# A recurrent attention and a routed expert layer on one core: q and k turned by products alone, gathers and weight loads in another order

## The chip, the cores and the metric

The kernel runs on one core of one Trainium2 chip. The metric is the device time of one execution in microseconds (us), lower is better. The kernel before was timed three times: 344.85, 353.26 and 343.91 us, a median of 344.85.

## What is computed

Two layers follow each other. The first is attention with a decaying state, for 4 batches, 8 heads, 768 positions and 64 values a head; the second sends each of the 3072 rows that come out of it either past the experts or to one of eight.

```python
def _attn_ref(q, k, v):                 # q, k, v: [4, 8, 768, 64]
    gamma = 1.0 - 2.0 ** (-5.0 - np.arange(H, dtype=np.float32))
    for t in range(S):
        state = gamma[None, :, None, None] * state + np.einsum('bhd,bhe->bhde', k[:, :, t], v[:, :, t])
        y[:, :, t] = scale * np.einsum('bhd,bhde->bhe', q[:, :, t], state)

def _moe_ref(x, w_skip, w_gate, w1, w2):   # x: [3072, 512], w1: [8, 512, 1024], w2: [8, 1024, 512]
    do_compute = x @ w_skip > 0
    out = x.copy()
    xc = x[do_compute]
    logits = xc @ w_gate
    e_idx = np.argmax(logits, axis=1)
    gate_w = softmax(logits)[e_idx]
    for e in range(E):
        mask = e_idx == e
        h = np.maximum(xc[mask] @ w1[e], 0.0)
        y[mask] = gate_w[mask, None] * (h @ w2[e])
    out[do_compute] = xc + y
```

## The kernel before, in words

**The attention stage** works on 16 pairs of heads (four batches of four pairs; index `i`), each with 768 positions in chunks of 128. One engine each has its part: SyncE loads the k, q and v of pair `i+4`; GpSimd (POOL) multiplies k and q of pair `i+2` with powers of the decay (`scale_rows`, line 94, tiles `ks` and `qs`); TensorE computes; ScalarE (ACT) and VectorE (DVE) carry results out of PSUM. The order of the instructions on each engine is the order in which the code is written (`manual_schedule`). One pass of the loop at line 433 issues on TensorE:

- `kv_states(i)`, line 232: 20 products of `ks` with v, 64x64, into the four 64x64 quarters of the array in turn. VectorE makes states `St` of them (lines 241 and 244).
- `scores(i, 0)`, line 270: 12 products. VectorE masks them into `ATm` (line 276).
- `rows_t(i+1, 0)`, lines 213 and 215: turns the k and a third of the q of the next pair, so that the position comes to lie along the free axis: 32 blocks of 64x64. ScalarE copies the result to `QKT` (line 217).
- `values(i-1)`, line 293, 24 products; ScalarE and VectorE copy a half each to `xT` (line 299).
- `rows_t(i+1, 1)`: the other 16 blocks.
- `scores(i, 1)` with the products of q and the states (line 250) in between; masked as above.
- `rows_x(i-1)`, line 317: turns the result back and multiplies it with the gate's columns at once. ScalarE copies to `xall` and `Lp`; after each fourth pair it sends the batch's rows to `out` (line 326).

The blocks of `rows_t` go through the four quarters of the array in turn. Where the result lies in the lower half of the PSUM partitions (`o == 0`), the block is turned by a transpose (line 213), otherwise by a product with the identity (line 215); so two transposes and two products take turns. A float32 product is two records in the trace, a transpose is one.

A batch that is complete goes through the gate in three following passes, on VectorE: the choice of the expert (`gate_a`), the place of each row in its expert's list (`gate_count`, `gate_b`, lines 364 to 395), and the table of the lists (`one_hots`, `table`, lines 404 to 420). The last batch does all three behind the last pair.

**The expert stage** begins with `slots`: row numbers (`gi` with empty slots set to row 0, for the gathers; `si` with empty slots set past the end, for the scatters) and the factors `g`. Each expert has 256 slots in two tiles of 128. POOL issues all 16 gathers of rows from `out` (line 498, a tile of its own each, `xg`), and between them the weights of experts 4 to 7 (`load_w`, lines 183 and 186; those of experts 0 to 3 were loaded during the attention). Then for each expert: `layer1` (line 522), `x_tr` of the next expert (lines 508 to 513: to bf16, turned), `layer2` (line 535), and for each of two tiles VectorE's weighted sum `yo` (line 540, four buffers) and POOL's scatter back to `out` (line 543). The scatters are declared free of each other, as they name distinct rows; of the gathers they are not, and since both work on `out`, a scatter waits for all gathers ahead of it. A loop behind this (line 585) takes further passes where an expert has over 256 rows; with these inputs it takes none.

The step from line 213 on is what the first part of the change touches, lines 477 to 563 the second.

Of the kernel before, what the change touches and what calls it, by code (L numbers as in the profile page):

```python
# [18 lines left out]
def kernel(  # L19
# [133 lines left out]
    w8 = poolC.tile([128, NCH * E], FP32, name="w8")  # L153
    vals = poolC.tile([128, NCHT, NV], BF16, name="vals")

    def gate_constants():
        ut_f = poolC.tile([128, 128], FP32, name="ut_f")
        make_upper_triangular(nc, ut_f[:, :], val=1.0, diag=False)
        iota_i = poolC.tile([128, CAP], I32, name="iota_i")
        G_.iota(iota_i[:, :], pattern=[[1, CAP]], base=0, channel_multiplier=0)  # L160
        w8_i = poolC.tile([128, NCH * E], I32, name="w8_i")
        G_.iota(w8_i[:, :], pattern=[[0, NCH], [-1, E]], base=E, channel_multiplier=0)
        chv_i = poolC.tile([128, NCHT], I32, name="chv_i")
        G_.iota(chv_i[:, :], pattern=[[1, NCHT // R], [0, R]], base=0, channel_multiplier=0)
        row_i = poolC.tile([128, NCHT], I32, name="row_i")
        G_.iota(row_i[:, :], pattern=[[0, NCHT // R], [1, R]], base=1, channel_multiplier=R)
        V_.tensor_copy(identb[:, :], ident[:, :])
        V_.tensor_copy(utb[:, :], ut_f[:, :])
        V_.memset(onesb[:, :], 1.0)
        V_.tensor_copy(iotab[:, :], iota_i[:, :])  # L170
        V_.tensor_copy(w8[:, :], w8_i[:, :])
        V_.tensor_copy(vals[:, :, 0], chv_i[:, :])
        V_.tensor_copy(vals[:, :, 1], row_i[:, :])
        V_.memset(Rsum[:, :], 0.0)
        V_.memset(Tsb[:, :], 0.0)
# [21 lines left out]
    def rows_t(i, m):  # L197
# [7 lines left out]
        for j in range(n):  # L205
            w, s_ = divmod(j0 + j, NCH)
            for c in range(2):
                cp = slice(64 * c, 64 * c + 64)
                for h in range(2):
                    o = 64 * (h ^ c)  # L210
                    dst, rows = ps[c][o : o + 64, j * 64 : (j + 1) * 64], (ks, qs)[w][i][cp, s_, h, :]
                    if o == 0:
                        PE.transpose(out=dst, in_=rows, identity=ident[cp, cp])  # L213
                    else:
                        PE.matmul(out=dst, lhsT=rows, rhs=ident[cp, cp], start=True, stop=True, skip_group_check=True)  # L215
        for c in range(2):
            A_.copy(  # L217
                out=QKT[i][:, j0 : j0 + n, 64 * c : 64 * c + 64],
# [214 lines left out]
    for i in range(NU):  # L433
# [6 lines left out]
        scale_rows(i + 2, 1, G_)  # L440
        if i == 0:
            gate_constants()
        for e, which in WEARLY.get(i, ()):
            load_w(e, which, poolW)
        rows_t(i + 1, 1)
# [29 lines left out]
    def slots():  # L475
# [2 lines left out]
        sh = [128, NST, E]  # L478
        tid = poolE.tile(sh, FP32, tag="tid", bufs=1, name="tid")
        V_.scalar_tensor_tensor(out=tid[:, :, :], in0=T[:, :, 0, :], scalar=256.0, in1=T[:, :, 1, :], op0=ALU.mult, op1=ALU.add)  # L480
        gi = poolE.tile(sh, I32, tag="gi", bufs=1, name="gi")
        V_.tensor_scalar(gi[:, :, :], tid[:, :, :], -1.0, 0.0, ALU.add, ALU.max)
        emp = poolE.tile(sh, FP32, tag="emp", bufs=1, name="emp")
        V_.tensor_scalar(emp[:, :, :], T[:, :, 1, :], 0.0, BIG, ALU.is_equal, ALU.mult)
        si = poolE.tile(sh, I32, tag="si", bufs=1, name="si")
# [1 line left out]
        g = poolE.tile(sh, FP32, tag="g", bufs=1, name="g")  # L487
        V_.tensor_tensor(g[:, :, :], T[:, :, 2, :], T[:, :, 3, :], ALU.add)
        V_.tensor_tensor(g[:, :, :], g[:, :, :], T[:, :, 4, :], ALU.add)  # L489
        return gi, si, g  # L490

    gi, si, g = slots()
    xg, xgT = {}, {}

    def gather(e, gi):
        for st in range(NST):
            t = poolE.tile([128, DM], FP32, tag=f"xg{e}_{st}", bufs=1, name="xg")
            G_.indirect_dma_start(  # L498
                out=t[:, :], out_offset=None, in_=out[:, :],
                in_offset=bass.IndirectOffsetOnAxis(ap=gi[:, st, e : e + 1], axis=0), bounds_check=N - 1, oob_is_err=False,  # L500
            )
            xg[e, st] = t

    def x_tr(e):
        xgT[e] = poolE.tile([128, NDB, CAP], BF16, tag="xgT", bufs=2, name="xgT")
# [20 lines left out]
            A_.activation(out=hT[:, 2 * f2 : 2 * f2 + 2, :], in_=ps[:, :, :], func=AF.Relu, bias=0.0, scale=1.0)  # L526
        return hT

    scatters = []

    def layer2(e, hT, si, g, first=False):
        for st in range(NST):
            ps = psE.tile([128, DM], FP32, tag="yps", bufs=2, name="yps2")
            for fb in range(NFB):
# [1 line left out]
                    out=ps[:, :], lhsT=hT[:, fb, st * 128 : (st + 1) * 128], rhs=w2b[e][:, fb, :],  # L536
                    start=(fb == 0), stop=(fb == NFB - 1),
                )
            yo = poolE.tile([128, DM], FP32, tag="yo", bufs=4, name="yo")
            V_.scalar_tensor_tensor(  # L540
                out=yo[:, :], in0=ps[:, :], scalar=g[:, st, e : e + 1], in1=xg[e, st][:, :], op0=ALU.mult, op1=ALU.add
            )
# [2 lines left out]
                in_=yo[:, :], in_offset=None, bounds_check=N - 1, oob_is_err=False,  # L545
            )
            if first:
                for o in scatters:
                    tc.declare_no_dep(sc.ins, o.ins, reason="the slots of a pass name distinct rows")
                scatters.append(sc)  # L550

    late = [(e, w) for e in range(4, E) for w in range(2)]
    for e in range(E):
        gather(e, gi)
        if e >= 1:
            load_w(*late.pop(0), poolX)
    load_w(*late.pop(0), poolX)
    x_tr(0)
    for e in range(E):
        hT = layer1(e)  # L560
        if e + 1 < E:
            x_tr(e + 1)
        layer2(e, hT, si, g, first=True)


    NPASS = (N + CAP - 1) // CAP - 1
# [18 lines left out]
    with tc.For_i(0, n_more) as _:  # L585
        V_.tensor_scalar(posT[:, :], posT[:, :], -float(CAP), None, ALU.add)
        V_.memset(Tsb[:, :], 0.0)
        for b in range(B):
            js = batch_js(b)
            table_add(table(js, one_hots(js, poolE), psE, "cnt", 1))  # L590
        gi2, si2, g2 = slots()
        for e in range(E):
            gather(e, gi2)
        for e in range(E):
            x_tr(e)
            layer2(e, layer1(e), si2, g2)

# [29 lines left out]
```

## Time and profile before

| | us |
|---|---|
| median of three executions | 344.85 |
| lowest, highest | 343.91, 353.26 |
| profiled execution, whole | 348.22 |
| its span in the trace | 346.1 |
| TensorE busy (share of the span) | 269.2 (78%) |
| TensorE's weight loads | 205.9 (60%) |
| VectorE busy | 132.6 (38%) |
| ScalarE busy | 74.2 (21%) |
| GpSimd busy | 90.1 (26%) |

The profile is of one execution, with times in us from the start of its span. Matmuls are pipelined: records overlap, and the pace is read from their starts. The attention stage goes to about 223 us, the expert stage from 232.86 to 336. A share of busy time is a mean over both. The chain of waits is followed back from the last instruction: at each step to what released it, or to the instruction before it on its engine; "issue" is time in which an engine waited for nothing that the profile shows. A wait for several semaphores is put down to the one that came last.

### The profile page before, as it was taken

What the parts mean: (1) busy time and instruction counts of PE and PEld (TensorE: products, weight loads), DVE (VectorE), ACT (ScalarE), POOL (GpSimd) and SP (SyncE); (2) the same over time, 40 slices, a digit from 0 to 9 for tenths busy, and PEclk for the clock granted to TensorE, in tenths of its full rate; (3) what the DMA queues carried; (4) which work ended last, traced back from release to release, by engine and by line L of the source; (5) the groups of instructions that cost most, each with busy time, mean ns of one, the idle gap of its engine ahead of it and who ended that gap; (6) DMA issues with size and microseconds to landing.
All of it is one profiled execution on the core that took longest, in us unless ns stands there. A gap on an engine that the chain in (4) does not pass through costs nothing.

```text
span 346.1 us, 10993 instructions
## 1 busy us (share of the span) xinstructions
PE 269.2 (78%) x4941; PEld 205.9 (60%) x4941; DVE 132.6 (38%) x423; ACT 74.2 (21%) x185; POOL 90.1 (26%) x95
## 2 busy tenths in 40 slices
PE   2999999999799989799999697624998300899960
PEld 1667877887687677577787476513666300466630
DVE  3444324424746532708533607462232001433320
ACT  2110322223132132123132121300222200022220
POOL 2723303321322141111430000007633212322220
PEclk9999989989999899769999878855899955699995
DMA  8995414438852259610589980046999995111110
GB/s 217 272 285 144 135 28 117 140 93 206 283 141 81 62 137 252 197 47 4 102 159 214 258 190 4 2 182 146 235 256 252 245 243 159 64 51 60 50 60 6
DMA packets 45202, 49.99 MB, mean 144 GB/s; under 512 B 2922, under 2 KB 39786, under 8 KB 43104
## 3 DMA queue, kind: packets, MB, share of 16 engines
q0 software_dynamic: 4864, 24.07, 30.2%
q1 hardware_dynamic: 38688, 18.90, 20.4%
q10 hardware_dynamic: 1600, 6.29, 4.6%
q8 instruction: 40, 0.66, 0.8%
q14 instruction: 10, 0.08, 0.1%
HBM read 56.64 MB, written 10.49 MB: 194 GB/s over the span
## 4 chain that ended last, share of the span: by engine, by line
PE 74%; DMA 9%; DVE 8%; issue 6%; ACT 1%; POOL 1%; POOLq 0%; DVEq 0%; ACTq 0%
PE tps L215 17%; PE tps L213 12%; PE atps L270 9%; PE yps L535 8%; PE hps L522 8%; PE yps L293 7%; DMA xg<-out_dram,gi 5%; PE kvps L232 4%; DMA out_dram<-yo,si 3%; PE tps L317 2%; PE yps L250 2%; DVE ATm L276 2%; PE xtp L512 2%; PE tabps L412 1%; DVE xb L508 1%
## 5 line engine op out<-in xcount | busy, mean ns | idle before, releaser
L276 DVE TENSOR_TENSOR ATm<-atps,maskc 128x384 f32<-128x384 f32 x64 | 32.7, 553 | 51.8 <-PE atps L270 51.4
L217 ACT COPY QKT<-tps 128x512 f32<-128x512 f32 (+1 forms) x64 | 27.6, 482 | 109.1 <-PE tps L215 109.1
L94 POOL TENSOR_TENSOR qs<-qw,tq 128x768 f32<-128x768 f32 x15 | 22.4, 1494 | 95.2 <-issue 80.2
L270 PE MATMUL atps<-QKT 64*64 64x128 f32 x768 | 41.6, 298 | 7.0 <-issue 4.7
L526 ACT ACTIVATE hT<-hps 128x512 bf16<-128x512 f32 x32 | 19.1, 597 | 86.3 <-PE hps L522 86.3
L215 PE MATMUL tps<-ident,ks 64*64 64x64 f32 x384 | 35.4, 265 | 0.5 <-issue 0.5
L512 PE MATMUL xtp<-identb,xb 128*128 128x128 bf16 x64 | 7.3, 244 | 36.3 <-DVE xb L508 36.3
L215 PE MATMUL tps<-ident,qs 64*64 64x64 f32 x384 | 35.2, 262 | 0.0
L270 PEld LDWEIGHTS atps<-QKT 64*64 64x64 f32 x768 | 29.5, 144 | 9.5 <-issue 5.3
L498 POOL DMA_INDIRECT xg<-out_dram,gi x16 | 16.3, 1020 | 68.9 <-DVE g L489 50.8
L213 PE MATMUL tps<-ident,ks 64*64 64x64 f32 x192 | 29.3, 259 | 6.2 <-POOL ks L94 6.2
L213 PE MATMUL tps<-ident,qs 64*64 64x64 f32 x192 | 33.1, 256 | 0.9 <-ACT QKT L217 0.9
L94 POOL TENSOR_TENSOR ks<-kw,tk 128x768 f32<-128x768 f32 x16 | 24.0, 1499 | 33.1 <-PE kvps L232 26.1
L522 PE MATMUL hps<-xgT,w1b 128*128 128x256 bf16 x256 | 32.1, 287 | 0.5 <-DVE xgT L513 0.5
L522 PEld LDWEIGHTS <-w1b 128*128 128x128 bf16 x256 | 30.1, 146 | 3.2 <-issue 0.7
L540 DVE SCALAR_TENSOR_TENSOR yo<-yps,g,xg 128x512 f32<-128x512 f32 x16 | 11.9, 750 | 48.7 <-DMA out_dram<-yo,si 28.3
L535 PE MATMUL yps<-w2b,hT 128*128 128x512 bf16 x128 | 30.2, 391 | 0.0
L293 PE MATMUL yps<-ATm,vn 64*64 64x128 f32 x768 | 29.9, 310 | 0.0
L244 DVE TENSOR_TENSOR St<-kvps,St 64x64 f32<-64x64 f32 x128 | 28.4, 222 | 3.0
L543 POOL DMA_INDIRECT out_dram<-yo,si x16 | 15.9, 992 | 48.2 <-DVE yo L540 35.5
L512 PEld LDWEIGHTS <-xb 128*128 128x128 bf16 x64 | 5.0, 121 | 38.1 <-DVE xb L508 38.1
L299 DVE COPY xT<-yps 128x384 f32<-128x384 f32 x16 | 8.9, 557 | 47.8 <-PE yps L293 47.7
(99 smaller groups left out, 319.8 us busy)
## 6 DMA issues: line engine op xcount, KB each, us to landing
w1b<-in_moe_w_dram POOLq DMA_DIRECT2D x8, 1024.0 KB
w2b<-in_moe_w_dram POOLq DMA_DIRECT2D x8, 1024.0 KB, 17.7
kw<-in_k_dram SPq DMA_DIRECT2D x16, 384.0 KB, 5.9
qw<-in_q_dram SPq DMA_DIRECT2D x16, 384.0 KB, 5.7
vn<-in_v_dram SPq DMA_DIRECT2D x16, 384.0 KB, 5.4
out_dram<-xall ACTq DMA_DIRECT2D x4, 1536.0 KB, 13.5
xg<-out_dram,gi POOLq DMA_INDIRECT x16, 12.7
out_dram<-yo,si POOLq DMA_INDIRECT x16, 2.6
```

The lines of the kernel that those rows point to most:

```text
L94: eng.tensor_tensor(o[:, :, :, :], rows, sc, ALU.mult)
L213: PE.transpose(out=dst, in_=rows, identity=ident[cp, cp])
L215: PE.matmul(out=dst, lhsT=rows, rhs=ident[cp, cp], start=True, stop=True, skip_group_check=True)
L217: A_.copy(out=QKT[i][:, j0 : j0 + n, 64 * c : 64 * c + 64], in_=ps[c][:, 0 : 64 * n].rearrange("p (j t) -> p j t", j=n),)
L244: V_.tensor_tensor(st[o : o + 64, ch, :], kv[o : o + 64, :], st[64 - o : 128 - o, ch - 1, :], ALU.add)
L270: PE.matmul(out=ps[t][cp, j, :], lhsT=QKT[i][hp, a * SPB + j, cp], rhs=QKT[i][hp, NCH + R * g : NCH + R * g + R, cp], start=True, stop=True,)
L276: V_.tensor_tensor(out=ATm[i, a][:, t, :, :], in0=ps[t][:, :, :], in1=maskc[:, a * SPB : (a + 1) * SPB, :, :].rearrange("p s r t -> p s (r ...
L293: PE.matmul(out=Y[i, c][64 * h : 64 * h + 64, g, :], lhsT=vn[i][cp, h * G + g, r * D : (r + 1) * D], rhs=ATm[i, a][cp, h ^ c, j, :], start ...
L512: PE.transpose(out=ps[:, db, :], in_=cols[:, db, :], identity=identb[:, :])
L522: PE.matmul(out=ps[:, f, :], lhsT=w1b[e][:, db, :].rearrange("p (c a) -> p a c", a=NFB)[:, fb, :], rhs=xgT[e][:, db, :], start=(db == 0), ...
L526: A_.activation(out=hT[:, 2 * f2 : 2 * f2 + 2, :], in_=ps[:, :, :], func=AF.Relu, bias=0.0, scale=1.0)
L535: PE.matmul(out=ps[:, :], lhsT=hT[:, fb, st * 128 : (st + 1) * 128], rhs=w2b[e][:, fb, :], start=(fb == 0), stop=(fb == NFB - 1),)
```

## The change

First, in `rows_t` the transposes are gone: every block is turned by a product with the identity. Second, the rows of the experts lie in eight fixed tiles `xrows`, two for each of four experts, set to zero once in pass 2 of the attention loop; expert `e` and expert `e + 4` share theirs. The gathers use `si`, so empty slots are left out and keep what was there. Only experts 0 to 3 are gathered at first, with two of the eight late weights in between; behind each expert's scatters stand the gather of the expert four further on, as long as there is one, and two late weights, as long as there are any. Scatters and gathers of this stage are declared free of each other, and `yo` has eight buffers.

```diff
+    xrows = [poolC.tile([128, DM], FP32, name=f"xrows{t}") for t in range(4 * NST)]
...
-                    dst, rows = ps[c][o : o + 64, j * 64 : (j + 1) * 64], (ks, qs)[w][i][cp, s_, h, :]
-                    if o == 0:
-                        PE.transpose(out=dst, in_=rows, identity=ident[cp, cp])
-                    else:
-                        PE.matmul(out=dst, lhsT=rows, rhs=ident[cp, cp], start=True, stop=True, skip_group_check=True)
+                    PE.matmul(
+                        out=ps[c][o : o + 64, j * 64 : (j + 1) * 64], lhsT=(ks, qs)[w][i][cp, s_, h, :],
+                        rhs=ident[cp, cp], start=True, stop=True, skip_group_check=True,
+                    )
...
+        if i == 2:
+            for t in xrows:
+                G_.memset(t[:, :], 0.0)
...
-        gi = poolE.tile(sh, I32, tag="gi", bufs=1, name="gi")
-        V_.tensor_scalar(gi[:, :, :], tid[:, :, :], -1.0, 0.0, ALU.add, ALU.max)
...
+    gathers, scatters = [], []
+
+    def free(ins, others):
+        for o in others:
+            tc.declare_no_dep(ins, o.ins, reason="the slots of a pass name distinct rows, empty ones none")
+
+    def gather(e, si, first=False):
         for st in range(NST):
-            t = poolE.tile([128, DM], FP32, tag=f"xg{e}_{st}", bufs=1, name="xg")
-            G_.indirect_dma_start(
+            t = xrows[(e % 4) * NST + st]
+            ga = G_.indirect_dma_start(
                 out=t[:, :], out_offset=None, in_=out[:, :],
-                in_offset=bass.IndirectOffsetOnAxis(ap=gi[:, st, e : e + 1], axis=0), bounds_check=N - 1, oob_is_err=False,
+                in_offset=bass.IndirectOffsetOnAxis(ap=si[:, st, e : e + 1], axis=0), bounds_check=N - 1, oob_is_err=False,
             )
             xg[e, st] = t
+            if first:
+                free(ga.ins, scatters)
+                gathers.append(ga)
...
-            yo = poolE.tile([128, DM], FP32, tag="yo", bufs=4, name="yo")
+            yo = poolE.tile([128, DM], FP32, tag="yo", bufs=8, name="yo")
...
             if first:
-                for o in scatters:
-                    tc.declare_no_dep(sc.ins, o.ins, reason="the slots of a pass name distinct rows")
+                free(sc.ins, scatters + gathers)
                 scatters.append(sc)
...
-    for e in range(E):
-        gather(e, gi)
-        if e >= 1:
+
+    def load_late(n):
+        for _ in range(min(n, len(late))):
             load_w(*late.pop(0), poolX)
-    load_w(*late.pop(0), poolX)
+
+    for e in range(4):
+        gather(e, si, first=True)
+        load_late(1 if e in (1, 2) else 0)
     x_tr(0)
     for e in range(E):
         hT = layer1(e)
         if e + 1 < E:
             x_tr(e + 1)
         layer2(e, hT, si, g, first=True)
+        if e + 4 < E:
+            gather(e + 4, si, first=True)
+        load_late(2)
```

In the order of TensorE's instructions, the kernel before has in a pass of the attention loop (`kvps` and `atps` are the PSUM tiles of the kv products and the scores, `tps` that of the turned blocks; x2 stands for two instructions of one line behind each other):

```order
L232 MATMUL kvps<-vn,ks 64x64 x20
L270 MATMUL atps<-QKT 64x128 x12
L213 MATMUL tps<-ident,ks 64x64
L215 MATMUL tps<-ident,ks 64x64 x2
L213 MATMUL tps<-ident,ks 64x64 x2
```

The changed kernel has in the same place of TensorE's order, and up to the second half of the scores (`yps` are the values):

```order
L233 MATMUL kvps<-vn,ks 64x64 x20
L271 MATMUL atps<-QKT 64x128 x12
L213 MATMUL tps<-ident,ks 64x64 x24
L213 MATMUL tps<-ident,qs 64x64 x8
L294 MATMUL yps<-ATm,vn 64x128 x24
L213 MATMUL tps<-ident,qs 64x64 x16
L271 MATMUL atps<-QKT 64x128 x8
```

Blocks stand in the same places; the runs of two became runs of 32 and 16.

In POOL's order the kernel before ends the issues of the expert stage so (`xg` are gathers, `w1b` and `w2b` weights, `yo` scatters):

```order
L498 DMA xg<-out_dram,gi 128x512 x2
L186 DMA w2b<-in_moe_w_dram 128x4096
L498 DMA xg<-out_dram,gi 128x512 x2
L183 DMA w1b<-in_moe_w_dram 128x4096
L186 DMA w2b<-in_moe_w_dram 128x4096
L543 DMA out_dram<-yo,si 3072x512 x16
```

The changed kernel has, in POOL's order from the first late weight (an expert 4's) to the last of expert 5's:

```order
L185 DMA w1b<-in_moe_w_dram 128x4096
L506 DMA xrows_159<-out_dram,si 128x512
L506 DMA xrows_160<-out_dram,si 128x512
L188 DMA w2b<-in_moe_w_dram 128x4096
L506 DMA xrows_161<-out_dram,si 128x512
L506 DMA xrows_162<-out_dram,si 128x512
L552 DMA out_dram<-yo,si 3072x512 x2
L506 DMA xrows_155<-out_dram,si 128x512
L506 DMA xrows_156<-out_dram,si 128x512
L185 DMA w1b<-in_moe_w_dram 128x4096
L188 DMA w2b<-in_moe_w_dram 128x4096
```

The first two scatters moved ahead of eight gathers and six weights.

## Rows read from the trace of the kernel before

**Rows 1.** Chain that ended last, on the page: share of the span by line.

```profile
PE tps L215 17%; PE tps L213 12%; PE atps L270 9%; PE yps L535 8%; PE hps L522 8%; PE yps L293 7%; DMA xg<-out_dram,gi 5%; PE kvps L232 4%; DMA out_dram<-yo,si 3%; PE tps L317 2%; PE yps L250 2%; DVE ATm L276 2%; PE xtp L512 2%; PE tabps L412 1%; DVE xb L508 1%
```

**Rows 2.** Timeline of TensorE, one pass: start, length, line, tiles, records, wait before.

```profile
101.95 0.86 PE L232 MATMUL kvps<-vn,ks 64*64 64x64 f32 x38 [0.30 <-DVE pm L380]
...
103.45 0.24 PE L213 MATMUL tps<-ident,ks 64*64 64x64 f32 x1
...
103.89 0.25 PE L213 MATMUL tps<-ident,ks 64*64 64x64 f32 x2
104.07 0.33 PE L215 MATMUL tps<-ident,ks 64*64 64x64 f32 x4
104.33 0.24 PE L213 MATMUL tps<-ident,ks 64*64 64x64 f32 x2
...
107.13 1.54 PE L293 MATMUL yps<-ATm,vn 64*64 64x128 f32 x48
...
110.52 0.67 PE L270 MATMUL atps<-QKT 64*64 64x128 f32 x16
```

**Rows 3.** Timeline of TensorE, the first 16 us.

```profile
8.44 0.48 PE L215 MATMUL tps<-ident,ks 64*64 64x64 f32 x4
...
9.09 0.48 PE L215 MATMUL tps<-ident,ks 64*64 64x64 f32 x4
...
15.29 1.44 PE L232 MATMUL kvps<-vn,ks 64*64 64x64 f32 x38
```

**Rows 4.** Windows: length, busy time of each engine, granted clock, DMA share, GB/s.

```profile
8.00:10.00 2.00, 2.00 (x22) 1.29 (x20) 1.97 (x9) 0.00 (x0) 1.28 (x1) 1.00 1.17 290
...
30.00:220.00 190.00, 175.93 (x4127) 139.19 (x4123) 89.25 (x293) 47.94 (x134) 40.23 (x32) 0.92 0.52 132
...
70.00:72.00 2.00, 2.00 (x35) 1.73 (x37) 0.00 (x0) 1.07 (x2) 0.00 (x0) 0.69 0.00 0
...
146.00:148.00 2.00, 2.00 (x22) 1.29 (x20) 0.00 (x0) 0.00 (x0) 0.00 (x0) 0.50 0.00 0
```

**Rows 5.** Timeline of TensorE: first and last of six gaps put down to "issue".

```profile
44.15 0.33 PE L215 MATMUL tps<-ident,ks 64*64 64x64 f32 x4 [0.51 <-issue]
...
195.47 0.87 PE L270 MATMUL atps<-QKT 64*64 64x128 f32 x19 [3.17 <-issue]
```

**Rows 6.** Timeline of TensorE, the last pass.

```profile
208.80 0.86 PE L232 MATMUL kvps<-vn,ks 64*64 64x64 f32 x38 [0.30 <-DVE pm L380]
...
213.92 1.37 PE L270 MATMUL atps<-QKT 64*64 64x128 f32 x13 [2.23 <-DVE ATm L276]
```

**Rows 7.** Timeline of VectorE, the last pass.

```profile
211.34 1.93 DVE L244 TENSOR_TENSOR St<-kvps,St 64x64 f32<-64x64 f32 x8
213.30 1.02 DVE L276 TENSOR_TENSOR ATm<-atps,maskc 128x384 f32<-128x384 f32 x2
```

**Rows 8.** Chain in order of time, the expert stage: start, us, what.

```profile
250.66 3.52 PE hps L522 x32
...
269.98 12.75 DMA xg<-out_dram,gi
...
318.71 3.53 PE hps L522 x32
...
327.18 3.53 PE hps L522 x32
330.71 3.45 PE yps L535 x16
```

**Rows 9.** Timeline of POOL.

```profile
39.09 1.50 POOL L94 TENSOR_TENSOR qs<-qw,tq 128x768 f32<-128x768 f32 x1 [6.88 <-PE tps L213]
...
181.55 0.54 POOL L186 DMA_DIRECT2D w2b<-in_moe_w_dram  x1
...
283.60 1.05 POOL L543 DMA_INDIRECT out_dram<-yo,si  x1 [11.43 <-DMA xg<-out_dram,gi]
```

**Rows 10.** Windows, as in rows 4: the end of the early weight loads.

```profile
206.00:208.00 2.00, 2.00 (x91) 2.00 (x92) 0.46 (x1) 0.52 (x2) 0.00 (x0) 1.00 0.08 16
```

More of the change, by code (lines that the diff above doesn't have):

```diff
@@ L489, in slots @@
         V_.tensor_tensor(g[:, :, :], g[:, :, :], T[:, :, 4, :], ALU.add)
-        return gi, si, g
-    gi, si, g = slots()
+        return si, g
+    si, g = slots()
     xg, xgT = {}, {}
-    def gather(e, gi):
+    gathers, scatters = [], []
[3 more added lines that the diff above has]
+    def gather(e, si, first=False):
         for st in range(NST):
-            t = poolE.tile([128, DM], FP32, tag=f"xg{e}_{st}", bufs=1, name="xg")
-            G_.indirect_dma_start(
+            t = xrows[(e % 4) * NST + st]
+            ga = G_.indirect_dma_start(
                 out=t[:, :], out_offset=None, in_=out[:, :],
-                in_offset=bass.IndirectOffsetOnAxis(ap=gi[:, st, e : e + 1], axis=0), bounds_check=N - 1, oob_is_err=False,
+                in_offset=bass.IndirectOffsetOnAxis(ap=si[:, st, e : e + 1], axis=0), bounds_check=N - 1, oob_is_err=False,
             )
             xg[e, st] = t
+            if first:
+                free(ga.ins, scatters)
+                gathers.append(ga)
     def x_tr(e):
@@ L527, in layer1 @@
         return hT
-    scatters = []
     def layer2(e, hT, si, g, first=False):
@@ L590 @@
             table_add(table(js, one_hots(js, poolE), psE, "cnt", 1))
-        gi2, si2, g2 = slots()
+        si2, g2 = slots()
         for e in range(E):
-            gather(e, gi2)
-        for e in range(E):
+            gather(e, si2)
             x_tr(e)
```

## The prediction

> **What bounds the kernel now.** I read the chain of waits first [rows 1]. Its two largest entries are one place, the turning of q and k (lines 213 and 215, 17% and 12% of the span); the two matrix products of the experts follow at 8% each, and two DMA entries, gathers 5% and scatters 3%, stand behind them. So the kernel has two stages with different limits. In the attention stage TensorE is busy nearly throughout; in the expert stage it stands still once for long.
>
> The timeline of TensorE shows one pass of the attention loop [rows 2]. The reader is to look at the starts, since records overlap. A pair of transposes holds TensorE from 103.89 to 104.07 (0.18 us), the four records behind it (two products with the identity, two records each) until 104.33 (0.26). The loop repeats this: 12 such groups of 0.44 in a pass. The two stretches of turning run from 103.45 to 107.13 and, behind the values (1.54, of which some 0.07 lie beneath what follows), from 108.60 to 110.52: 3.68 + 1.92 = 5.60 us. The same view has the same kind of product elsewhere: the kv products take ks as the stationary operand, 64x64, in the same four quarters of the array, and 38 records of them take 0.86 us. Less the last record's own length (0.24, as a single one has), that is 0.62/37 = 17 ns a record, against 0.26/4 = 65 ns for the products that stand between transposes. So the turning pays for the alternation, not for the work.
>
> The first 23 us show it at another pace [rows 3]: groups start 0.65 apart (8.44 to 9.09), and kv records come (1.44 - 0.32)/37 = 30 ns apart. [...] Between 70 and 72 us the clock fell to a mean of 0.69 while TensorE did nothing but turn, without an idle moment. Over 30 to 220 us the mean is 0.92, a loss of 190 x 0.08 = 15 us.
>
> What else holds the attention stage: six gaps that the profile puts down to "issue", 0.5 to 3.2 us each, 9.2 us in sum; the first and the last stand in [rows 5]. And VectorE in the passes behind a gate: the last pass has no turning left to do, yet the second half of its scores starts 213.92 - 208.80 = 5.12 us after its kv products, having waited 2.23 us for VectorE's masking [rows 6], which could start only at 213.30 behind the gate's steps and the states [rows 7].
>
> In the expert stage the chain [rows 8] runs expert 1 from 250.66, then stands at 269.98 on a gather (12.75 us), until POOL issues its first scatter at 283.60 after 11.43 us of waiting for a gather [rows 9]; undisturbed experts come 327.18 - 318.71 = 8.47 us apart, the last takes 3.53 + 3.45.
>
> **The change part by part.** The sum is made against the profiled execution: 346.1 us of span and 348.22 us in all, 1% above the median of 344.85.
>
> *Turning, passes 1 to 14.* 24 transposes become products, so 48 products, 96 records, stand without a break. No row shows such a run. Nearest below is the kv pace, 17 ns, so 96 x 17 = 1.63 us; above, the pace of the products as they now stand, 65 ns, so 6.24 us, 0.6 more than now. I take 17, since operand, shape and quarters of the array are the same and only the identity is new. Saved: 14 x (5.60 - 1.63) = 55.5 us (by the upper bound -9).
>
> [...]
>
> *Turning, the first two sets.* At the lower pace 12 x 0.65 = 7.8 against 96 x 0.030 = 2.9 us: twice 4.9, so 9.8. Input DMAs and the ScalarE copies, which already make TensorE wait there, could take 3 of it.
>
> *What is late next.* A pass of TensorE shrinks to some 7 us. Its second scores then come 1.50 + 1.09 + 1.47 + 0.54 = 4.6 us after the kv products (kv with first scores, 64 records, values, 32 records), while VectorE allows them at about 4.2 in a plain pass (kv 0.86, a first state and eight more 2.2, masking 1.02 [rows 7]), and at 5.1 behind a gate's second part [rows 6]; when one of its small copies takes long it is more. I charge 1 us for three passes behind the gate's first part and 1.25 for two behind the second: -5.5 in sum (bounds 0 and -15).
>
> *Clock.* Of the 15 us, half should come back, +7: less time is spent turning, but new waits of 1 to 2 us give other occasions (bounds -15, if every such wait is followed by some 5 us at the lower level, and +15).
>
> *"Issue" gaps.* They fall where DMA is full. As many instructions are now used up in less time, and the same transfers fill a larger share of it: -4 (bounds +9, none left, and -15).
>
> *Rows and weights.* POOL's order is shown with the change. In before every scatter waits for all 16 gathers, and these stand between weight loads in one queue; now the scatters are declared free of them. Eight weights behind 16 gathers become two between the first eight gathers, and two behind the scatters of experts 0, 1 and 2. Are they there in time? The last four of the early loads were issued up to 181.55 and DMA was quiet at 206 [rows 9, 10], so a load takes about 6.2 us. Those of expert 5 start at about 252 in the old time and are there at 264, of 6 at 277, of 7 at 289; they are wanted at 284, 293 and 301. Expert 4's gather, issued before them, is wanted three experts later. What remains is 250.66 + 6 x 8.47 + 3.53 + 3.45 = 308.5 against 330.71 + 3.45 = 334.16: 25.7 us saved; the indices for the gathers come one small VectorE step later, so 25.5. If a load took twice as long, two experts would wait and some 12 be given back.
>
> *At no cost.* No row has a memset of 512 columns; scaling 768 takes 1.50 us, so eight memsets take at most 8 x 1.0. They stand behind the qs of pair 4, ahead of which POOL had been idle for 6.88 us [rows 9], and the ks behind them is wanted more than a pass later. Without this cover TensorE would wait up to 8 us once. Skipped empty rows and more yo buffers: 0 (a gain of less than 1).
>
> Sum: 55.5 + 9.8 - 5.5 + 7 - 4 + 25.5 = 88. On the profiled execution 260; I say 262, since the waits that I could not see are more likely to be missing than gains are.
>
> **The rivals.**
> *A: the gain is eaten by what comes next.* VectorE's waits at their bound (-15 rather than -5.5), no clock regained (0 for +7) and gaps at 8 rather than 4: 262 + 20 = 282. For it: [rows 5, 6]; against: VectorE has 38% of the span and only three of sixteen passes carry each gate step.
> *B: the products run slower than kv's, at 30 ns,* say because the identity is read by all: 16 x 96 x 13 ns = +20, part of it beneath VectorE's waits: 276. Against it: nothing in kv's rows differs but that operand.
> *C: the scatters stay bound,* by another wait in POOL's queue, where each DMA also waits for an older one: the 25.5 go, 287. Against it: before, each of the older ones has landed by the times above.
> [...]
>
> **How the numbers follow.** Forecast 0.62 (its own range 252 to 272); A 0.17, B 0.09, C 0.08, D 0.04. The range for 8 in 10 goes down to 249, where clock and gaps are regained too (0.08 lie below), and up to 285, which takes in A and B; C and D are left out. [...] Faster 0.95, within 2% 0.02, slower 0.03.
>
> **What would show it.** Right: line 213 alone, 768 further product records, its starts 17 ns apart and some 1.1 + 0.55 us a pass; kv starts some 7 us apart in plain passes; waits of TensorE for the masking in the passes behind gates; first scatter right behind expert 0's second product, and experts 8.5 us apart from first to last with no gap over 1 us. Wrong: records 30 ns apart or more (B, D); "issue" gaps over 15 us in sum or a lower mean clock (A); a scatter that waits for DMA (C).

## The result, and the profile after

The changed kernel takes 295.18 us, the median of four executions (294.91 to 299.14), beside 349.06 us for the kernel before: a ratio of 0.860, 95% interval 0.850 to 0.870. It is faster, as forecast, but by 54 us and not by 88; 262 was wrong, and the range ended 10 us too early. The profiled execution was the longest of the four: 299.14 us, with a span of 297.2, against 348.22 and 346.1 before.

Where the 48.9 us between the two spans come from is read from three places in TensorE's timeline: the second pass's first kv product, the last row product of the attention, and the last product of the last expert ([rows 8] for before). The first two of them in the kernel before:

```profile
29.30 0.48 PE L232 MATMUL kvps<-vn,ks 64*64 64x64 f32 x4
...
221.95 1.15 PE L317 MATMUL tps<-IW,xT 64*64 64x73 f32 x48 [0.61 <-ACT xT L299]
```

and in the changed kernel, with the last passes between them:

```profile
17.32 0.27 PE L233 MATMUL kvps<-vn,ks 64*64 64x64 f32 x1
...
192.31 1.13 PE L271 MATMUL atps<-QKT 64*64 64x128 f32 x16 [2.12 <-DVE ATm L277]
...
199.07 1.14 PE L318 MATMUL tps<-IW,xT 64*64 64x73 f32 x48 [0.61 <-ACT xT L300]
```

| stretch | before | after | saved | forecast |
|---|---|---|---|---|
| up to the second pass's kv product | 29.3 | 17.3 | 12.0 | 9.8 |
| from there to the last row product's end | 193.8 | 182.9 | 10.9 | 53 (55.5 - 5.5 + 7 - 4) |
| from there to the last expert's end | 111.1 | 85.3 | 25.7 | 25.5 |
| the rest | 11.9 | 11.7 | 0.3 | 0 |

Two of three terms came in as forecast. All that is missing, 42 us, is missing in passes 1 to 15 of the attention. The page of the changed kernel (busy times; granted clock and DMA share in 40 slices; the queue that brings instructions; the chain by engine and by line, which answers to [rows 1]; a q behind an engine's name is its sequencer):

```profile
PE 204.0 (69%) x5325; PEld 175.2 (59%) x5325; DVE 134.9 (45%) x422; ACT 74.3 (25%) x185; POOL 94.4 (32%) x103
...
PEclk9998979995979897799897796897559999999995
DMA  7999753289624579720869993005398799995110
...
q8 instruction: 43, 0.70, 1.0%
...
PE 59%; issue 18%; DVE 13%; DMA 3%; SPq 3%; ACT 2%; POOL 1%; ACTq 0%; POOLq 0%
PE hps L533 10%; PE yps L544 9%; PE atps L271 9%; PE yps L294 8%; PE tps L213 8%; PE yps L251 4%; PE tps L318 4%; DVE ATm L277 3%; PE kvps L233 2%; DMA qw<-in_q_dram 2%; SPq L83 2%; PE xtp L523 2%; PE tabps L413 1%; DVE xb L519 1%; DVE St L245 1%
```

The turning, 29% of the chain before, is 8% now. But 18% of it, some 53 us, is "issue": time in which the engine waited for nothing that the profile shows. The view of TensorE's waits from 10 to 200 us says on which lines (line and what was waited for: us in total, times, longest):

```profile
PE tps L213 <- issue: 24.0, 11, 4.5
PE yps L294 <- issue: 8.0, 5, 3.0
PE atps L271 <- DVE ATm L277: 5.6, 3, 2.4
PE atps L271 <- issue: 5.5, 3, 2.7
PE tps L318 <- issue: 2.4, 4, 1.0
PE kvps L233 <- issue: 2.1, 2, 1.7
PE yps L251 <- issue: 2.0, 2, 1.4
PE tps L213 <- POOL ks L94: 1.9, 1, 1.9
```

The same wait stands on six lines, whatever tile they write; so it belongs to no tile. The timeline of TensorE shows where it falls. The turning itself has the forecast pace (the row at 64.72: 48 records, (0.92 - 0.22)/47 = 15 ns apart). Then it stops in the middle of a set:

```profile
63.37 0.22 PE L318 MATMUL tps<-IW,xT 64*64 64x73 f32 x1 [0.98 <-issue]
63.38 0.86 PE L233 MATMUL kvps<-vn,ks 64*64 64x64 f32 x38
64.02 0.33 PE L271 MATMUL atps<-QKT 64*64 64x128 f32 x2
64.06 0.23 PE L233 MATMUL kvps<-vn,ks 64*64 64x64 f32 x2
64.12 0.82 PE L271 MATMUL atps<-QKT 64*64 64x128 f32 x22
64.72 0.92 PE L213 MATMUL tps<-ident,ks 64*64 64x64 f32 x48
65.43 0.45 PE L213 MATMUL tps<-ident,qs 64*64 64x64 f32 x14
69.83 0.26 PE L213 MATMUL tps<-ident,qs 64*64 64x64 f32 x1 [3.95 <-issue]
...
70.00 2.77 PE L294 MATMUL yps<-ATm,vn 64*64 64x128 f32 x45
```

From one stop to the next the counts give 1 + 38 + 2 + 2 + 22 + 48 + 14 = 127 records. Counted through the whole attention, every gap but one (at 173.19, four records too early) lies on one grid, 127 or 128 records, or a multiple of that, behind the one before, and so do the six gaps of the kernel before, of which [rows 5] has two. With its weight load each record is two instructions, so 128 records are 256 instructions. The queue of the page that carries instructions has 43 packets and 0.70 MB for 10,650 instructions of TensorE (5325 matmul records and as many weight loads): 16 KB a packet. The times of these packets in the trace settle what the gaps are: each of the 25, but for the one at 173.19, ends 1.2 to 1.7 us after one of them has landed, and so do the six of the kernel before.

Behind this gap the clock is low: the 45 records from 70.00 take 2.77 us, and the windows (length, busy time and instructions of each engine, granted clock, DMA share, GB/s) give 0.50 for the 4 us after it. Of the ten stretches at 0.50 between 20 and 200 us, 3.4 or 6.8 us long each, eight began in such a gap of 1.9 us or more, or up to 1.5 us behind one (at 27.0, 37.3, 68.0, 95.3, 112.4, 119.2, 160.1 and 180.6); of the other two one began behind a gap of 0.62 us (at 81.6) and one behind none (at 146.5).

```profile
70.00:72.00 2.00, 2.00 (x42) 2.00 (x45) 0.00 (x0) 0.58 (x1) 0.00 (x0) 0.50 0.89 281
72.00:74.00 2.00, 2.00 (x63) 2.00 (x59) 0.56 (x1) 0.92 (x3) 0.25 (x1) 0.50 1.05 415
...
30.00:200.00 170.00, 120.19 (x4284) 111.14 (x4277) 85.93 (x280) 46.23 (x130) 39.57 (x36) 0.88 0.58 146
```

The expert stage did what was said of it. The chain there runs through TensorE from expert to expert, 8.4 to 8.9 us apart from the second expert on (the first interval, 216.02 to 227.32, was 11.3, with a granted clock of 0.52 from 204 to 221 us), and no wait of a scatter for a gather is left; POOL's one scatter that waited for a weight delays nothing on the chain:

```profile
261.62 3.53 PE hps L533 x32
...
270.10 3.53 PE hps L533 x32
...
278.57 3.53 PE hps L533 x32
282.10 3.45 PE yps L544 x16
```

```profile
28.56 3.78 POOL L446 MEMSET xrows<- 128x512 f32 x8
...
269.43 0.98 POOL L552 DMA_INDIRECT out_dram<-yo,si  x1 [5.01 <-DMA w2b<-in_moe_w_dram]
```

### The profile page after: what moved, and what is told of

It reads as the page before. It is cut to its first block, busy times and chain, and to the rows that moved or that the text cites. A ratio compares the mean times of both kernels' runs of the same rounds, so it can differ in the third digit from the quotient of the medians.

```text
span 297.2 us, 11761 instructions
## 1 busy us (share of the span) xinstructions
PE 204.0 (69%) x5325; PEld 175.2 (59%) x5325; DVE 134.9 (45%) x422; ACT 74.3 (25%) x185; POOL 94.4 (32%) x103
## 4 chain that ended last, share of the span: by engine, by line
PE 59%; issue 18%; DVE 13%; DMA 3%; SPq 3%; ACT 2%; POOL 1%; ACTq 0%; POOLq 0%
PE hps L533 10%; PE yps L544 9%; PE atps L271 9%; PE yps L294 8%; PE tps L213 8%; PE yps L251 4%; PE tps L318 4%; DVE ATm L277 3%; PE kvps L233 2%; DMA qw<-in_q_dram 2%; SPq L83 2%; PE xtp L523 2%; PE tabps L413 1%; DVE xb L519 1%; DVE St L245 1%
## 5 line engine op out<-in xcount | busy, mean ns | idle before, releaser
L271 PE MATMUL atps<-QKT 64*64 64x128 f32 x768 | 45.9, 307 | 11.2 <-DVE ATm L277 5.6
L271 PEld LDWEIGHTS atps<-QKT 64*64 64x64 f32 x768 | 33.5, 152 | 13.5 <-DVE ATm L277 7.2
L213 PE MATMUL tps<-ident,qs 64*64 64x64 f32 x768 | 26.2, 251 | 19.0 <-issue 17.7
L213 PEld LDWEIGHTS tps<-ident,qs 64*64 64x64 f32 x768 | 23.0, 161 | 20.3 <-issue 18.5
L506 POOL DMA_INDIRECT xrows<-out_dram,si x16 | 16.6, 1036 | 57.2 <-DVE g L490 52.6
L294 PEld LDWEIGHTS yps<-ATm,vn 64*64 64x64 f32 x768 | 29.0, 161 | 9.1 <-issue 9.1
L245 DVE TENSOR_TENSOR St<-kvps,St 64x64 f32<-64x64 f32 x128 | 28.4, 222 | 3.0
L213 PE MATMUL tps<-ident,ks 64*64 64x64 f32 x768 | 19.2, 241 | 14.6 <-POOL ks L94 8.1
L213 PEld LDWEIGHTS tps<-ident,ks 64*64 64x64 f32 x768 | 17.8, 152 | 15.6 <-POOL ks L94 8.3
L318 PE MATMUL tps<-IW,xT 64*64 64x73 f32 x768 | 22.6, 244 | 3.0 <-issue 2.4
L324 ACT COPY xall<-tps 128x384 f32<-128x384 f32 x32 | 15.4, 485 | 34.1 <-PE tps L318 34.1
```

What stands on the lines that cost most here:

```text
L213: PE.matmul(out=ps[c][o : o + 64, j * 64 : (j + 1) * 64], lhsT=(ks, qs)[w][i][cp, s_, h, :], rhs=ident[cp, cp], start=True, stop=True, ski ...
L245: V_.tensor_tensor(st[o : o + 64, ch, :], kv[o : o + 64, :], st[64 - o : 128 - o, ch - 1, :], ALU.add)
L271: PE.matmul(out=ps[t][cp, j, :], lhsT=QKT[i][hp, a * SPB + j, cp], rhs=QKT[i][hp, NCH + R * g : NCH + R * g + R, cp], start=True, stop=True,)
L294: PE.matmul(out=Y[i, c][64 * h : 64 * h + 64, g, :], lhsT=vn[i][cp, h * G + g, r * D : (r + 1) * D], rhs=ATm[i, a][cp, h ^ c, j, :], start ...
L318: PE.matmul(out=ps[h][cp, s_ * XW : (s_ + 1) * XW], lhsT=xT[i][hp, s_, cp], rhs=IW[hp, p, :], start=True, stop=True, skip_group_check=True,)
L506: ga = G_.indirect_dma_start(out=t[:, :], out_offset=None, in_=out[:, :], in_offset=bass.IndirectOffsetOnAxis(ap=si[:, st, e : e + 1], axi ...
```

## The experiments

Theory S (supply): TensorE's instructions come in blocks of 128 records; beside quiet DMA engines a block arrives every 3.5 to 4.0 us, beside full ones every 5 to 9 (an estimate from the 4.8 to 7.5 measured in the changed kernel), and the faster turning now waits for them. Rivals: the gaps belong to TensorE itself (its clock, its pace), or DMA traffic alone makes them. The table counts, in each profiled execution, TensorE's gaps of 0.35 us and more in the attention that have no releaser. Such a sum is good to a few us: in the changed kernel it leaves out 2.2 us at 175.69 that stand on the grid, and the same attention gave 41.7, 39.9 and 38.4 in changed, turn_alone and after_pair.

| kernel | records in the attention | gaps: number, us | attention ends | whole, median (executions) |
|---|---|---|---|---|
| before | 4473 | 6, 9.2 | 223.1 | 349.06 (4) |
| changed | 4857 | 25, 41.7 | 200.2 | 295.18 (4) |
| turn_alone | 4857 | 25, 39.9 | 194.3 | 319.96 (4) |
| expert_alone | 4473 | 5, 8.7 | 225.3 | 323.66 (4) |
| x_half | 4473 | 16, 26.9 | 194.8 | 292.89 (4) |
| x_double | 5625 | 27, 47.8 | 215.6 | 313.96 (4) |
| t_half | 4089 | 11, 18.7 | 204.7 | 298.24 (4) |
| dma_quiet | 4857 | 24, 35.0 | 192.6 | 292.19 (1) |
| held | 4857 | 19, 26.6 | 180.1 | 308.12 (1) |
| dma_quiet_timed | 4857 | 20, 27.9 | 186.4 | 286.13 (4) |
| quiet_x | 4473 | 17, 24.4 | 185.7 | 285.09 (4) |
| after_pair | 4857 | 21, 38.4 | 193.9 | 294.92 (4) |
| quiet_pair | 4857 | 16, 29.2 | 186.7 | 285.36 (4) |

### The two parts apart

turn_alone is the kernel before with the products only, expert_alone the changed kernel with the transposes back:

```diff
-                    if o == 0:
-                        PE.transpose(out=dst, in_=rows, identity=ident[cp, cp])
-                    else:
-                        PE.matmul(out=dst, lhsT=rows, rhs=ident[cp, cp], start=True, stop=True, skip_group_check=True)
+                    PE.matmul(
+                        out=ps[c][o : o + 64, j * 64 : (j + 1) * 64], lhsT=(ks, qs)[w][i][cp, s_, h, :],
+                        rhs=ident[cp, cp], start=True, stop=True, skip_group_check=True,
+                    )
```

> The kernel before with the products for the transposes, the expert stage as before. If the two parts of the change add up, as the traces say (attention 22.9 us shorter, expert stage 25.8), this run saves about 23: 326 us of 349. With the supply theory (TensorE's instructions come in blocks of 128 matmul records, each not sooner than 3.7 to 4.0 us after the one ahead, and 5 to 9 while DMA is full) the waits that the profile calls issue sum to some 40 us here as in the changed kernel, and stand 128 records apart or a multiple of it. If they came from the new expert stage's larger program, they would be at 10 us.

> The changed kernel with the transposes back: gathers, weights and fixed tiles alone. Additive: about 26 saved, 323 us; issue waits at some 9 us as before. If the eight memsets or the constant tiles cost the attention something, it is more than 323 by that.

Measured: 319.96 us (317.63 to 322.56), ratio 0.918, interval 0.907 to 0.930; and 323.66 (314.52 to 332.39, too wide for a ratio). Beside 348.37 for the kernel before these are 28.4 and 24.7 us, 53.1 together, against 53.9 for both at once: as far as the 18 us between the executions of expert_alone allow, the parts add. turn_alone saved 6 us more than expected, and its attention ended 6 us sooner than the changed kernel's. The gaps come with the products (39.9 us) and not with the new order of gathers and weights (8.7). From the attention's end to the last expert turn_alone needs 111.2 us, as before, and expert_alone 84.2.

### Fewer and more records

x_half makes the row products (line 318) over all 128 columns of `xT` at once, so half as many; x_double cuts each in two along its output:

```diff
-            for c in range(2):
-                cp = slice(64 * c, 64 * c + 64)
-                for h in range(2):
...
-                        out=ps[h][cp, s_ * XW : (s_ + 1) * XW], lhsT=xT[i][hp, s_, cp], rhs=IW[hp, p, :],
+            for h in range(2):
...
+                    out=ps[h][:, s_ * XW : (s_ + 1) * XW], lhsT=xT[i][hp, s_, :], rhs=IW[hp, p, :],
```

```diff
+                    for u in (slice(0, 37), slice(37, XW)):
...
+                            out=ps[h][cp, s_ * XW + u.start : s_ * XW + u.stop], lhsT=xT[i][hp, s_, cp], rhs=IW[hp, p, u],
```

> The changed kernel with rows_x as 12 products of 128 stationary columns instead of 24 of 64: the same results with 384 matmul records less in the attention, 3 blocks of 128. TensorE's own work doesn't shrink (each product fills twice the columns of the array). Supply theory: 3 x 4 to 5 us less, 280 to 284 us. Rival (TensorE's work, or waits on other engines that the profile doesn't name): 293 to 298.

> The changed kernel with each product of rows_x cut in two by its moving columns (37 and 36 of 73): the same columns, 768 matmul records more, 6 blocks. Supply theory: 6 x 4 to 5 more, 319 to 325 us. Rival (the records' own time): at 5 to 10 ns more of each, 4 to 8 us, 299 to 303.

Measured: x_half 292.89 us (ratio 0.842, interval 0.833 to 0.852), x_double 313.96 (0.903, 0.898 to 0.908). The gaps moved the way that S says, down by 14.8 us (S: 12 to 15) and up by 6.1, not much more than the same attention's own spread. The times did not reach S's numbers: x_half came out at the lower end of its rival's, x_double between the two. In both the records' own time had been mis-sized. In x_half the product over 128 columns is slow on TensorE:

```profile
58.58 1.56 PE L316 MATMUL tps<-IW,xT 64*128 64x73 f32 x24
60.07 0.86 PE L233 MATMUL kvps<-vn,ks 64*64 64x64 f32 x38
```

24 records take 60.07 - 58.58 = 1.49 us, 62 ns each; the 48 that they replace take 1.14 - 0.22 = 0.92 us (the row at 199.07). Over 16 passes that is 9.1 us more, and the attention ends only 5.4 us earlier: 9.4 of the 14.8 were given back. In x_double 768 records at 17 ns are 13 us, and with 6.1 more of gaps 19.2, near the 18.8 measured. The instruction queue's packets settle what a block is. Of x_half, then of x_double:

```profile
q8 instruction: 40, 0.66, 0.9%
```

```profile
q8 instruction: 49, 0.80, 1.0%
```

1152 records more are 9 packets more: 128 records to a packet.

t_half takes 768 records out at the turning: one product over 128 columns turns both heads, for which k and q are loaded with the heads of their lower half exchanged (more input DMAs).

```diff
-                for h in range(2):
-                    o = 64 * (h ^ c)
-                    PE.matmul(
-                        out=ps[c][o : o + 64, j * 64 : (j + 1) * 64], lhsT=(ks, qs)[w][i][cp, s_, h, :],
...
+                PE.matmul(
+                    out=ps[c][:, j * 64 : (j + 1) * 64], lhsT=(ks, qs)[w][i][cp, s_, :, :],
```

> The changed kernel with the two heads of a chunk turned by one product of 128 stationary columns instead of two of 64; the upper half of the partitions holds the heads in the other order, by two more input DMAs for k and for q. 768 records less, 6 blocks. x_half showed records with 128 columns at 62 ns, so a set takes 48 x 62 ns = 3.0 us instead of 1.6, some +20 us of TensorE in all; supply theory: the waits fall by 6 x 5 = 30 from 42, some of TensorE's longer time hidden in what is left; 280 to 292 us. Rival (TensorE's time alone): 295 + 20 = 315.

Measured: 298.24 us, from 291.07 to 304.16, so not told from the changed kernel; S had 280 to 292, its rival 315. The gaps fell to 18.7 us, the lowest of all kernels with products alone. But the 24 k records of a set take 58 ns each (62.10 to 63.49), 1.39 us, twice what the 48 that they replace took (65.43 - 64.72 = 0.71 us), and the first kv product comes at 13.95 instead of 10.07 us.

### The supply by itself

burst puts 512 products of the turning's kind (1024 records), which wait for nothing and whose result nobody reads, behind the last pass; burst_dma does so with four of the early weight loads held back until then (one execution each, 324.95 and 325.51 us).

```diff
+    for n in range(512):
+        c, h = (n // 2) % 2, n % 2
+        cp, o = slice(64 * c, 64 * c + 64), 64 * (h ^ c)
+        m = (n // 4) % 8
+        PE.matmul(
+            out=bps[c][o : o + 64, m * 64 : (m + 1) * 64], lhsT=IW[cp, m % NP, 0:64], rhs=ident[cp, cp],
+            start=True, stop=True, skip_group_check=True,
+        )
```

```diff
+    late_t = poolC.tile([128, 4], FP32, name="late_t")
+    G_.tensor_copy(late_t[:, :], ATm[NU - 1, 1][:, 1, 0, 0:4])
+    for e, which in ((2, 0), (2, 1), (3, 0), (3, 1)):
+        load_w(e, which, poolW)
```

> The changed kernel with 512 more 64x64 products (1024 matmul records, 8 blocks of 128) between the last pair's values and its rows_x, where DMA is quiet; they wait for nothing and nobody reads them. This measures the supply by itself. Supply theory: a wait called issue each 128 records, a block each 3.7 to 4.0 us, so 29 to 32 us for the 1024. Rival (TensorE's pace alone): 15 to 17 ns a record, 15 to 18 us without such waits.

> The same 512 products, while four weight loads (1 MB each, those of experts 2 and 3, held back until the last scores are masked) fill the DMA queues. Supply theory with DMA's part in it: blocks 5 to 9 us apart while the loads run (some 25 us), then 3.7 to 4.0: 36 to 50 us for the 1024. If the supply doesn't depend on the load of the queues: 29 to 32 as in burst. Rival (pace alone): 15 to 18.

The burst in TensorE's timeline, and its window:

```profile
195.12 2.16 PE L469 MATMUL bps<-ident,IW 64*64 64x64 f32 x136
198.31 2.10 PE L469 MATMUL bps<-ident,IW 64*64 64x64 f32 x128 [1.02 <-issue]
202.03 2.10 PE L469 MATMUL bps<-ident,IW 64*64 64x64 f32 x128 [1.63 <-issue]
205.76 2.09 PE L469 MATMUL bps<-ident,IW 64*64 64x64 f32 x128 [1.63 <-issue]
209.22 2.09 PE L469 MATMUL bps<-ident,IW 64*64 64x64 f32 x128 [1.36 <-issue]
...
195.00:222.00 27.00, 16.85 (x1040) 15.79 (x1032) 0.56 (x1) 0.48 (x1) 0.00 (x0) 1.00 0.02 5
```

Neither rival can be the cause here: the clock is 1.00 throughout, the DMA share 0.02, the products have no input to wait for, and yet TensorE stands still for 10 of 27 us. It takes exactly 128 records in 2.1 us (16.4 ns each) and then waits until 3.45 to 3.73 us have gone by since the block before. The packets' times in the trace divide this interval: a packet starts 1.0 to 1.7 us after TensorE has begun on the block ahead, takes 0.9 to 1.4 us, and TensorE goes on 1.3 to 1.6 us after it has landed. The burst took 26.7 us; S had expected 29 to 32, its rival 15 to 18; the interval is a little shorter than S had it. The same beside the weights:

```profile
188.48 2.16 PE L473 MATMUL bps<-ident,IW 64*64 64x64 f32 x136
194.12 2.71 PE L473 MATMUL bps<-ident,IW 64*64 64x64 f32 x128 [3.47 <-issue]
200.59 3.69 PE L473 MATMUL bps<-ident,IW 64*64 64x64 f32 x128 [3.77 <-issue]
206.78 6.67 PE L473 MATMUL bps<-ident,IW 64*64 64x64 f32 x256 [2.50 <-issue]
213.96 2.10 PE L473 MATMUL bps<-ident,IW 64*64 64x64 f32 x128 [0.51 <-issue]
217.42 2.09 PE L473 MATMUL bps<-ident,IW 64*64 64x64 f32 x128 [1.36 <-issue]
...
188.00:208.00 20.00, 10.26 (x462) 9.75 (x456) 0.56 (x1) 0.48 (x1) 0.00 (x0) 0.68 0.99 206
```

With a DMA share of 0.99 the blocks stand 6.47 and 6.19 us apart, once the loads are over 3.46 again. The packet itself is no slower in these two intervals, 0.97 us, but it starts only 4.0 us after TensorE has begun on the block ahead. In all it took 34.4 us, a little less than the 36 to 50 expected, because the loads lasted for only half of it. The clock falls too, to a mean of 0.68 in that stretch.

### The weights' share

dma_quiet takes the early weight loads out of the attention's passes and puts them behind it in the code; dma_quiet_timed and quiet_pair are the same kernel:

```diff
-        for e, which in WEARLY.get(i, ()):
-            load_w(e, which, poolW)
...
+    for e in range(4):
+        load_w(e, 0, poolW)
+        load_w(e, 1, poolW)
     for e in range(4):
         gather(e, si, first=True)
```

held loads them only when the last pass's masked product is there (with `late_t` as above), quiet_x is dma_quiet with x_half's edit.

> The changed kernel with the eight early weight loads moved from the attention to the head of the expert stage: the attention keeps its input loads and its stores. The whole gets longer, the expert stage waits for its weights; what counts is the attention's end (200.2 us in the changed kernel) and the sum of the issue waits in it (41.7). Supply theory: blocks that come in 5 to 9 us now come in some 4, so the waits fall to 15 to 25 us and stay at multiples of 128 records; attention's end 175 to 188. If full DMA queues alone made them: below 6 us, end at 160 to 168. If neither: 42 and 200.

Measured: 292.19 us, the attention's end at 192.6 and gaps of 35.0, more than both theories gave. The edit did less than it says: POOL, which runs ahead of TensorE, issued the loads from 143.6 us on, so the last quarter of the attention still ran beside them, with blocks 6.2 to 6.8 us apart (DMA share 0.83 from 140 to 200 us).

> The changed kernel with all eight weight loads of experts 0 to 3 held until the last pass's masked product exists, so that no weight moves beside the attention. In the run with the loads merely moved to the end of the attention's code they still ran from 147 us on; its stretch 36 to 140 us, free of them, had 3063 records in 104 us, 34 ns a record, against 2801, 37 ns, in the changed kernel. Theory S (blocks of 128 records arrive every 3.7 to 4.0 us beside quiet DMA engines and every 5 to 9 beside full ones): the attention goes on at 34 ns a record to its end: from 36 us with some 4,100 records left, 36 + 4,100 * 0.034 = 175, so it ends at 172 to 183 us (200.2 in the changed kernel, 192.6 with the loads moved), with no wait over 3 us after 36 us but where input rows fill the DMA engines; the expert stage then waits for its weights and the whole is 285 to 300. Rival (the waits have nothing to do with the weights' transfers): it ends at 192 to 200 and the gaps over 3 us stay.

Measured: attention's end 180.1 us, gaps 26.6, none above 3 us, as S has it; its rival had 192 to 200. The windows of the end of the attention, of held and then of quiet_pair, have a DMA share of 0.19 and 0.96:

```profile
140.00:180.00 40.00, 31.26 (x1105) 28.53 (x1097) 23.20 (x79) 11.97 (x34) 6.31 (x11) 0.91 0.19 55
```

```profile
140.00:187.00 47.00, 31.82 (x1007) 29.09 (x999) 21.20 (x73) 10.54 (x32) 5.95 (x9) 0.85 0.96 213
```

That is 36 ns a record against 47, with the clock at 0.91 and 0.85. The whole was 308.12 us, above the expected 285 to 300: the weights now collide with the store of the attention's rows (21.8 us on the chain) and the first gathers (19.2).

> The kernel with the early weight loads behind the attention's code, once more with rounds. One look gave 292.2. S: 290 to 293, 1% under the changed kernel, since seven of its attention's 24 waits shrink. Rival (noise of one run): 295 to 299.

> The changed kernel with both edits that took waits away: the key rows' product over 128 columns at once (384 records fewer) and the early weight loads behind the attention's code. Alone they gave 292.9 and 292.2. If their gains add (S: fewer blocks, and each sooner): 288 to 291, attention ending at 187 to 190. Rival (both take away the same waits, or TensorE gives back the rest since the 128-column records take 62 ns): 291 to 294.

Measured: 286.13 us (284.02 to 290.08; ratio 0.830, interval 0.809 to 0.851) and 285.09 (283.08 to 288.0; 0.824, 0.808 to 0.839). Both are below what either theory gave, and they are not told apart, so nothing shows that the two gains add. The gaps fell only from 27.9 to 24.4 us between them.

> The changed kernel once more, on the same chip and beside the version with the early weight loads moved, since the two were measured on different days' chips so far (295.2 and 286.1 us). S: 293 to 298, 2 to 4% above the other. Rival (the difference is between chips): within 1% of it.

> The version with the early weight loads behind the attention's code, beside the changed kernel. S: 285 to 290, 2 to 4% below it. Rival (the difference is between chips): within 1%.

Measured on one chip, side by side: 294.92 us (292.80 to 298.92) and 285.36 (283.33 to 291.42), 3.2% less, and the four executions of the one do not overlap those of the other. So the version with the early loads behind the attention's code beats both kernels. The windows from 36 to 140 us, of after_pair and then of quiet_pair, show it in the stretch that the loads left:

```profile
36.00:140.00 104.00, 77.25 (x2895) 71.47 (x2894) 56.97 (x180) 31.91 (x90) 30.71 (x23) 0.90 0.57 151
```

```profile
36.00:140.00 104.00, 80.33 (x3126) 74.47 (x3128) 60.29 (x195) 34.12 (x95) 29.93 (x20) 0.93 0.44 129
```

8% more records in the same time, with the DMA share down from 0.57 to 0.44.

## Why the prediction was wrong

*Turning, right.* 17 ns a record were forecast from the kv rows, 15 were measured; line 213 alone is left, and turn_alone gives the gain with nothing else changed. With this fall B and D, for which the records were to come 30 ns apart or more.

*First two sets, right:* 12.0 us for 9.8.

*What is late next, right in kind.* 5.5 us were charged for VectorE; its waits (lines 277, 405 and 381) grew by 3.3, from 4.6 to 7.9 us, and the last pass's 2.23 became 2.12. One wait for POOL's `ks`, 1.9 us, was not foreseen.

*Experts, right:* 25.7 us for 25.5, by the mechanism described; C falls. The memsets took 3.78 us, within the bound, and nothing waited for them.

*"Issue" gaps, the step that failed.* The prediction said that these gaps "fall where DMA is full" and charged 4 us more, 15 at most. They grew by 32.5, so 28.5 were missed here. The sign was right and the cause was half right: full DMA engines lengthen them (from block to block 6.2 to 6.5 us in burst_dma), but held shows 26.6 us with no weights in the way, and burst shows them at a DMA share of 0.02. What lies beneath is a floor: 304 records a pass (4857/16) are 2.4 blocks, at 3.5 to 4.0 us 8 to 9.5 us a pass, and at the 6 us beside full DMA engines 14. The forecast's sum came to (193.8 - 53)/15 = 9.4 us a pass, which the supply alone takes beside quiet engines. Its "some 7 us" for a pass lies below that; two passes did come to 7.3 and 7.4 us (kv starts 10.07 to 17.32 and 100.72 to 108.16), but the measured mean is 182.9/15 = 12.2. In the kernel before a pass took about 13 us for 2.2 blocks, so the supply was in time but for six gaps, and hidden.

*Clock, wrong in sign.* Half of the 15 us was to come back, +7; that half was an estimate, and no run shows it. Over 30 to 200 us the mean is 0.88, a loss of 170 x 0.12 = 20 us, 5 worse than before [rows 4], so 12 were missed (11, if the time in which TensorE stands still is left out of both losses). The rows from 70.00 on show the occasion that the bound of -15 named: a gap of 4 us and then a granted clock of 0.50 for 4 more.

28.5 and 12 make 40.5 of the 42 us that are missing in passes 1 to 15. TensorE's busy and idle time in this stretch agree with that: busy it was 179.1 us before and 128.7 after, so 50.4 were saved where 55.5 + 7 had been forecast; idle it was 14.7 and 54.2, so 39.5 were added for a forecast of 5.5 + 4. Some 6 of the 42 belong to the one execution profiled: in after_pair, the same kernel, the attention ended at 193.9 with gaps of 38.4. Rival A was right in kind, and its test (gaps over 15 us in sum, a lower mean clock) is the one that was met; but its 282 had the gaps at 8, and its largest term, 9.5 us more of waits for VectorE, did not come.

What the other transfers add can be told gap by gap from the packets' times. In the changed kernel, where two gaps are 127 or 128 records apart, the packet started 1.0 to 1.4 us after TensorE had begun on the block ahead if the interval was up to 4.0 us (at a DMA share of 0.02 to 0.60), and 2.3 to 5.0 us after it if the interval was 4.8 to 7.5 (at 0.67 to 1.13). The early weights' part is about 15 us of 41.7, by held. Whether the clock would be full without the gaps was not tried: in all kernels with products alone the mean over 30 to 200 us stayed at 0.86 to 0.91.

## What to carry to other kernels

Before crediting faster small products, divide the records of a stretch by 128 and multiply by the interval of blocks (here 3.5 to 4.0 us, and 6.2 to 6.5 at a DMA share of 0.99): in burst 1024 records, eight blocks, took 26.7 us, though 64x64 records at 16.4 ns used a block up in 2.1 us. Gaps that the profile puts down to nothing are worth counting in records: here a constant distance, 127 or 128, named the cause, and the kernel before already showed it. Where a stretch is at this floor, move bulk transfers out of it (quiet_pair took 285.36 us, after_pair 294.92), but not on top of a store or gather that the next stage waits for (held took 308.12).

## What the runs showed of the hardware

- TensorE's instructions came in packets of 16 KB, 128 matmul records with their weight loads (x_half to x_double: 1152 records more, 9 packets more). Where the supply alone held TensorE, its blocks started 3.45 to 3.73 us apart, and TensorE used one up in 2.1 us (burst).
- Each of TensorE's gaps ended 1.2 to 1.7 us after such a packet had landed (changed kernel, all but one of 25). A packet took 0.9 to 1.4 us, and it started 1.0 to 1.7 us after TensorE had begun on the block ahead (burst).
- At a DMA share of 0.99 the blocks started 6.2 to 6.5 us apart (burst_dma), in the changed kernel's attention 4.8 to 7.5 us apart at shares of 0.67 to 1.13. There the packets took no longer (0.97 us in burst_dma), but started later: 4.0 us after TensorE had begun on the block ahead (burst_dma), up to 5.0 in the attention.
- The records of float32 products (two each) with a 64x64 stationary operand, four quarters in turn, came 15 to 17 ns apart (changed kernel, kernel before), those with 64x128 62 ns (x_half) and 58 (t_half). Halving the number of records so gave 292.89 and 298.24 us, beside 295.18.
